# Attention scores from raw fp32 keys and queries, two heads on row halves, and all softmax weights turned as fp32r

## The chip, the cores and the metric

The kernel runs on one core of one Trainium2 chip. The metric is the device time in microseconds (us), the median of three runs. The kernel before takes 802.15 us (801.47 to 803.35).

## The reference

Three layers follow one another; everything is float32.

```python
# attention: batch 2, 8 heads, 576 tokens, head size 64
scores = scale * np.matmul(q, k.transpose(0, 1, 3, 2))
kth = np.partition(scores, -32, axis=-1)[..., -32:-31]     # the 32nd largest of each row
scores = np.where(scores >= kth, scores, -1e9)
attn = softmax(scores)                                     # written out in the reference
x = np.matmul(attn, v)                                     # then as 1152 tokens x 512
# experts: 4 of them, 512 -> 1024 -> 512
out += p[:, e:e+1] * (np.maximum(x @ w1[e], 0.0) @ w2[e])
# gated layer: 512 -> 1536 (twice) -> 512
y = ((x @ w_a) * (x @ w_b)) @ w_out
```

## The kernel before, in words

**Tokens.** The 1152 tokens are nine tiles of 128: four of each batch element, and one mixed tile with the last 64 tokens of both. `GROUPS` cuts the nine tiles into groups of 1, 2, 3 and 3; the last group holds two plain tiles and the mixed one. A group's attention runs over four pairs of heads, so there are 36 steps n = 0 to 35, each one tile with two heads; group 1 is n = 4 to 11, group 2 is n = 12 to 23, group 3 is n = 24 to 35.

**One step of attention.** `scores` (line 874) multiplies queries by keys into PSUM. ScalarE copies the scores to SBUF. `masked` (line 908) finds the 32nd largest of each row on VectorE: four MAX8 and three MATCH_REPLACE8 for each head (lines 930 and 936), all of 576 columns. ScalarE makes the softmax (lines 960, 965, 976) in a tile `e`. `weigh` (line 983) turns the weights on TensorE, nine 128x128 transposes a step, ScalarE copies them out, and when the last tile of a pair of heads is there, TensorE multiplies them by V (line 1033): ten pairs of matmuls a tile, the two heads of a pair on column halves of the array.

**Number formats.** A plain fp32 matmul is split into two instructions by the compiler, an fp32r one is a single instruction. Before the change the scores use fp32r. Keys and queries are split into a high part (ScalarE, line 623) and a remainder (GpSimd or VectorE, lines 625 and 627); both parts stand in the 128 rows of the array for one head, turned by fp32r transposes, and each query tile is multiplied twice, the second time with its halves swapped (`qa` and `qb`). So a plain tile has eight matmuls of 288 columns a step, and the mixed tile sixteen, with `qm` as its padded queries. The weights of steps n < 24 are turned in fp32. Those of n = 24 to 35 (`MOVED`) are first copied by DMA into an fp32r tile (`ers`) and turned there.

**The layers behind attention.** Group 0 goes through the experts in plain fp32 (`plain`), the others in a high and low split (`experts`, lines 1100 and 1115: in the trace `ps<-xs,mid_again` for the first matrix and `ps<-mid_again` for the second). Each weight unit is split by `w_unit`: ScalarE makes the high part (line 1073); the remainder comes from GpSimd, or from VectorE where `late` says so (lines 1076 and 1078):

```python
            late = 2 if c == len(GROUPS) - 1 and e >= 2 else 0
...
            lo = vector(dve(1024), lambda: sub(nc.vector), 500 + s if late > 1 else -100, [hi], [u, r], port=True)
        else:
            lo = gpsimd(pool_(1024), lambda: sub(nc.gpsimd), -100, [hi], [u, r])
```

The gated layer follows when all groups are through.

**What sets the order.** Every operation is given to a planner (`Plan`) with an engine, a duration and a key. The planner plays the whole program through with these durations, picks on each engine the ready operation with the smallest key, and the result is one fixed order for each engine. Score and attention work has keys near n, expert work has keys from 1000, evictions and remainders have negative keys. An engine then runs its list strictly in order. All transfers are issued by SyncE.

Of the kernel before, what the change touches and what calls it, by code (L numbers as in the profile page):

```python
# [21 lines left out]
MIX = "mix"  # L22
# [9 lines left out]
STORED, STORE_AT, STORE_KEY = 3, 10, 2.5  # L32
MOVED = (*range(24,36),)
# [43 lines left out]
class Buffer:  # L77
    def __init__(self, slots, need):
        self.slots, self.need, self.slot, self.users = slots, need, None, 0

    @property
    def ap(self):
        a = self.slots.aps[self.slot]
        return a[0][a[1]] if isinstance(a, tuple) else a

# [29 lines left out]
class Plan:  # L115
# [82 lines left out]
    def order(self):  # L198
# [34 lines left out]
        def place(t):  # L233
# [3 lines left out]
            if t.n != s.next:  # L237
                return None
            for i in sorted(s.free):
# [17 lines left out]
        def pick(engine):  # L257
# [6 lines left out]
            while ready_:  # L264
# [4 lines left out]
                ok = y is None or free[y.engine] <= now  # L269
                for t in op.tiles:  # L270
                    if t.slot is None and (t.slots in stuck or place(t) is None):
                        if t.n == t.slots.next:
                            stuck.add(t.slots)
                        ok = False
                if ok:
# [108 lines left out]
TURN_R, TURN_F, TOP, REPLACE = 88, 109, 662, 732  # L384
AV, SWITCH = 1092, 350

# [15 lines left out]
def body(tc, q, k, v, probs, w1, w2, wa, wb, wo, out):  # L402
# [58 lines left out]
    qm = const("qm", [128, 2, 2, 2, 128], F32R)  # L461
# [6 lines left out]
    kscr = dr.tile([B, HP, 2 * D, 2, S], F32, name="kscr")  # L468
    qscr = dr.tile([len(SIZES), HP, 2 * D, 2 * 3 * 128], F32, name="qscr")
    wscr = dr.tile([F2 // 256, 128, 2048], F32, name="wscr")  # L470

    big = Region("big", 10752, F32R)
    krems = big.slots("krem", 1, 1024)
    kspls = big.slots("kspl", 1, 2 * M4 * 2 * D)
    big.at = 2304
    bts = big.slots("bt", 4, 2 * S)
    qspls = big.slots("qspl", 1, 2 * 3 * 2 * D)
    qas = big.slots("qa", 2, 2 * 3 * 128)
    qbs = big.slots("qb", 1, 2 * 3 * 128)
    qts = big.slots("qt", 1, 2 * 3 * 128)  # L480
    big.at = 0
    ers = big.slots("er", 2, 2 * S)
    ers.rank = 0.5
# [10 lines left out]
    low = Region("low", 9228 + 3 * DM, F32)  # L494
    kraws = low.slots("kraw", 2, 2 * M4 * D)
    vts = low.slots("vt", 4, 2 * M4 * D)
    qraws = low.slots("qraw", 1, 2 * 3 * D)
    es = low.slots("e", 3, 2 * S)
# [4 lines left out]
    krraws = kraws  # L503
    low.at = 9228
# [3 lines left out]
    low.at = 9228  # L508
# [4 lines left out]
    big.again()  # L513
# [4 lines left out]
    ress.append(low.slots("res2", 1, DM))  # L518
    draws = low.slots("draw", 2, 1024)
    dcs = low.slots("dc", 2, 512)  # L520
# [1067 lines left out]
```

## Time and profile before

| | |
|---|---|
| median of the runs | 802.15 us (801.47 to 803.35) |
| profiled execution | 803.23 us, of which the span 801.2 us |
| mean granted TensorE clock | 0.987 |
| PE busy | 776.7 us, 97% |
| DVE busy | 706.7 us, 88% |
| ACT busy | 526.0 us, 66% |
| POOL busy | 338.0 us, 42% |
| chain that ended last | PE 67%, DVE 23%, ACT 4% |

The span is what the profiler saw on the core; 2.0 us of the profiled time lie around it. PE is TensorE, DVE VectorE, ACT ScalarE, POOL GpSimd, SP SyncE with the DMA queue. A PE row's length covers overlapping matmuls and a modelled end, so the real step of a PE group is read from its start to the start of the next group.

### The profile page before, as it was taken

The page shows a single profiled execution, that of the slowest core. Times are in us where ns is not written, and L with a number is a line of the kernel's source. Part 1 is how long each engine was busy: PE and PEld are TensorE (multiplying, and loading weights), DVE is VectorE, ACT ScalarE, POOL GpSimd, SP SyncE. Part 2 cuts the span into 40 slices and gives each one's busy share as a digit, 9 for nine tenths or more (in the row PEclk, how much of TensorE's full clock was granted, in tenths as well). Part 3 has the DMA queues.
Part 4 walks back from the last instruction along what each step waited for, and adds up shares of the span by engine and source line. Part 5 has one row for each costly group of instructions (what it writes and reads, how often), then busy time and mean ns, then how long its engine had stood idle before and what let it go on. Part 6 is the DMA issues. An engine that isn't in the chain of part 4 may idle for free.

```text
span 801.2 us, 14455 instructions
## 1 busy us (share of the span) xinstructions
PE 776.7 (97%) x5221; PEld 702.3 (88%) x5221; DVE 706.7 (88%) x1398; ACT 526.0 (66%) x926; POOL 338.0 (42%) x318
## 2 busy tenths in 40 slices
PE   6699999999999999999999999999999999999998
PEld 5587787799999989999999998999898989899996
DVE  7999999999999999999943676789788989999965
ACT  5899888999989898977774545566554533334210
POOL 4312113566765734535364656422224334333320
PEclk8799999999999999999999999999999999999999
DMA  5987997957657575763445544598631313304013
GB/s 170 328 278 228 301 313 238 271 187 248 211 173 227 178 216 172 227 191 129 145 154 168 185 129 147 158 324 296 223 142 54 106 53 106 131 28 158 1 53 119
DMA packets 98008, 143.57 MB, mean 179 GB/s; under 512 B 11792, under 2 KB 66064, under 8 KB 96400
## 3 DMA queue, kind: packets, MB, share of 16 engines
q1 hardware_dynamic: 97936, 142.65, 54.9%
q8 instruction: 41, 0.67, 0.3%
q14 instruction: 31, 0.25, 0.1%
HBM read 117.46 MB, written 14.42 MB: 165 GB/s over the span
## 4 chain that ended last, share of the span: by engine, by line
PE 67%; DVE 23%; ACT 4%; issue 3%; DMA 2%; POOL 1%; POOLq 0%; SPq 0%; DVEq 0%
PE ps L569 64%; DVE low L930 10%; DVE low L936 9%; PE ps L572 3%; DVE mid_again L1146 1%; DMA big<-big 1%; ACT low L965 1%; DVE low L1171 1%; ACT low L960 1%; POOL mid_again L1074 0%; DMA low<-in_v_dram 0%; ACT big L623 0%; ACT lowa L903 0%; POOL big L627 0%; DVE xs L1052 0%
## 5 line engine op out<-in xcount | busy, mean ns | idle before, releaser
L569 PE MATMUL ps<-mid_again 128*128 128x512 f32 x1092 | 261.7, 392 | 0.0
L569 PEld LDWEIGHTS ps<-mid_again 128*128 128x128 f32 x1092 | 201.5, 188 | 38.9 <-ACT raw L1521 0.2
L1074 POOL TENSOR_TENSOR mid_again<-raw,mid_again 128x1024 fp32r<-128x1024 f32 x80 | 192.6, 2418 | 65.8 <-ACT mid_again L1073 64.3
L569 PE MATMUL ps<-xs,mid_again 128*128 128x384 f32 (+1 forms) x1152 | 194.1, 320 | 0.1
L569 PEld LDWEIGHTS ps<-xs,mid_again 128*128 128x128 f32 x1152 | 182.4, 189 | 2.4 <-issue 0.5
L930 DVE MAX8 low<-low 128x8 f32<-128x576 f32 x216 | 154.5, 750 | 0.0
L1073 ACT ACTIVATE mid_again<-raw 128x1024 fp32r<-128x1024 f32 x96 | 101.1, 1063 | 32.4 <-PE ps L569 20.3
L936 DVE MATCH_REPLACE8 low<-low 128x576 f32<-128x576 f32 x144 | 106.5, 746 | 0.0
L1390 POOL TENSOR_TENSOR low<-low 128x512 int32<-128x512 int32 x36 | 50.7, 1407 | 116.6 <-DVE low L1387 80.9
L569 PE MATMUL ps<-xs,big 128*128 128x320 f32 (+1 forms) x576 | 86.4, 297 | 0.0
L569 PEld LDWEIGHTS ps<-xs,big 128*128 128x128 f32 x576 | 80.2, 190 | 0.8
L1146 DVE SCALAR_TENSOR_TENSOR mid_again<-ps,mid_again 128x384 fp32r<-128x384 f32 (+1 forms) x96 | 48.5, 508 | 32.9 <-ACT mid_again L1142 32.7
L569 PE MATMUL ps<-lowa_again,big 128*128 128x320 f32 (+1 forms) x432 | 66.4, 297 | 0.8 <-ACT rest L1488 0.6
L1142 ACT ACTIVATE mid_again<-ps 128x384 fp32r<-128x384 f32 (+1 forms) x96 | 44.0, 458 | 32.7 <-PE ps L569 29.9
L569 PEld LDWEIGHTS ps<-lowa_again,big 128*128 128x128 f32 x432 | 60.6, 190 | 2.2 <-ACT rest L1488 0.9
L960 ACT ACTIVATE low<-lowa,low 128x576 f32<-128x576 f32 x72 | 54.4, 781 | 4.7 <-POOL low L950 4.6
L976 ACT ACTIVATE low<-low 128x576 f32<-128x576 f32 x72 | 53.5, 778 | 5.1 <-DVE low L973 4.6
L965 ACT ACTIVATE low<-low 128x576 f32<-128x576 f32 x72 | 56.1, 783 | 0.2 <-POOL low L954 0.2
L936 DVE MATCH_REPLACE8 low<-low,lowa 128x576 f32<-128x576 f32 x72 | 53.2, 746 | 0.0
L1016 ACT ACTIVATE lowa<-ps 128x512 f32<-128x512 f32 x72 | 46.3, 654 | 9.4 <-PE ps L572 8.9
L930 DVE MAX8 low<-lowa 128x8 f32<-128x576 f32 x70 | 50.0, 748 | 0.7 <-ACT lowa L903 0.7
L1479 DVE TENSOR_TENSOR low<-ps,low 128x256 f32<-128x256 f32 (+1 forms) x105 | 43.2, 445 | 7.6 <-PE ps L569 6.5
(121 smaller groups left out, 1115.8 us busy)
## 6 DMA issues: line engine op xcount, KB each, us to landing
raw<-in_moe_w_dram SPq DMA_DIRECT2D x116, 512.0 KB, 4.1
big<-kscr SPq DMA_DIRECT2D x20, 576.0 KB, 5.0
big<-low SPq DMA_DIRECT2D x24, 288.0 KB, 3.3
low<-in_v_dram SPq DMA_DIRECT2D x24, 256.0 KB, 3.8
low<-in_moe_w_b_dram SPq DMA_DIRECT2D x12, 512.0 KB, 3.7
low<-in_moe_w_a_dram SPq DMA_DIRECT2D x12, 512.0 KB, 3.6
low<-in_moe_w_out_dram SPq DMA_DIRECT2D x12, 512.0 KB, 4.4
wscr<-big SPq DMA_DIRECT2D x6, 1024.0 KB, 5.9
```

The lines of the kernel that those rows point to most:

```text
L569: nc.tensor.matmul(out, l, r, **kw)
L930: 62 + 1.04 * width, lambda at=at, cs=cs: nc.vector.max(m8v()[:, x, cs], at()), key + 0.02 * r, [done],
L936: lambda at=at, cs=cs: nc.vector.match_replace(out=src[1](), in_to_replace=m8v()[:, x, cs], in_values=at(), imm_value=LOW),
L960: S, lambda x=x, s=s: nc.scalar.activation(ev(x), s.ap, AF.Prelu, bias=endv()[:, x, 1:2], scale=scale, alpha=STEEP),
L965: lambda x=x: nc.scalar.activation(ev(x), ev(x), AF.Exp, bias=endv()[:, x, 0:1], accum_out=sums.ap[:, x:x + 1]),
L976: S, lambda x=x: nc.scalar.activation(ev(x), ev(x), AF.Copy, scale=sums.ap[:, x:x + 1]),
L1016: w, lambda j=j, w=w, at=at: nc.scalar.activation(p.ap[:, j * MAIN:j * MAIN + w], at.ap.rearrange("p b n -> p (b n)")[:, j * (MAIN - 128): ...
L1073: hi = scalar(1024, lambda: nc.scalar.activation(u.ap[:, 0:1024], r.ap, AF.Copy), 500 + s, [ld], [u, r], sbuf=True)
L1074: sub = lambda eng: eng.tensor_tensor(u.ap[:, 1024:2048], r.ap, u.ap[:, 0:1024], op=ALU.subtract)
L1142: n, lambda h=h, p=p: nc.scalar.activation(h.ap[:, 0:n], p.ap[:, 0:n], AF.Relu), -1000, [o], [h, p]
L1146: lambda h=h, p=p: nc.vector.scalar_tensor_tensor(h.ap[:, n:2 * n], p.ap[:, 0:n], 0.0, h.ap[:, 0:n], op0=ALU.max, op1=ALU.subtract),
L1390: return gpsimd(pool_(512), lambda: nc.gpsimd.tensor_tensor(t().bitcast(I32), fold(c.ap.bitcast(I32)), fold(lowv().bitcast(I32)), op=ALU.a ...
```

## The change

- Keys and queries are no longer split. The raw keys of a pair of heads are loaded side by side, turned by six plain fp32 transposes a block, and evicted in one copy: head 0 stands in rows 0 to 63, head 1 in rows 64 to 127. Queries are turned in the same way, one transpose a tile.
- `scores` makes both heads in one step: four fp32 matmuls of 288 columns, each on one row half. In the mixed tile each is cut once more into two 64-column halves, one for each batch element: eight matmuls.
- All 36 steps' weights are turned as fp32r. The tile `e` is asked for a second time at the same address with the type fp32r (`Typed`); a GpSimd memset of one column behind its end stands for the new tile's write, and the transposes wait for it. The copies of `MOVED`, the mirrored queries and the stored queries go.
- `late`: VectorE makes the weight remainders of all of group 3 and of experts 2 and 3 of group 2; in all 48 of 96 instead of 16 of 96.

```diff
-MOVED = (*range(24,36),)
...
+LATE = 2
...
+    def keys(b, h2, key):
...
+        for m0, m1 in ((0, 2), (2, M4)) if first_ else ((0, M4),):
+            for i in range(2):
+                lds.append(load(
+                    lambda i=i, m0=m0, m1=m1: rv()[:, m0:m1, i], lambda i=i, m0=m0, m1=m1: main_rows(k, b, h)[:, i, m0:m1],
+                    key - 2, (), [rt], 32768 * (m1 - m0),
+                ))
+        if first_:
+            for c in range(B):
+                for x in range(B):
+                    rs = slice((x + c) % B * REM, ((x + c) % B + 1) * REM)
+                    krem_done.append(load(
+                        lambda c=c, rs=rs: krem[c].ap[rs].rearrange("p (h d) -> p h d", d=D), lambda x=x: last_rows(k, x), key - 1.98, (), [krem[c]], 131072,
+                    ))
...
+            tr(a[:, 0:128], kr[0], ident)
+            for m in range(M4):
+                tr(a[:, (1 + m) * 128:(2 + m) * 128], rt.ap[:, m * 128:(m + 1) * 128], ident)
+            tr(a[:, 640:768], kr[1], ident)
+
+        o = tensor(6 * TURN_F, turn, key + 0.02, lds + krem_done + [ready], [at, rt] + krem)
...
+            for i, t in enumerate(pair.tiles):
+                tr(a()[:, i * 128:(i + 1) * 128], qrem[:, h:h + 2].rearrange("p h d -> p (h d)") if t == MIX else rq.ap[:, i * 128:(i + 1) * 128], ident)
...
+        parts = [(slice(0, 128), t[0])] if t != MIX else [(slice(b * REM, (b + 1) * REM), b) for b in range(B)]
...
             for c in range(2):
-                for m_, (a, kt) in enumerate(parts):
-                    for lh in range(2):
+                for j in range(2):
+                    for rs, b in parts:
+                        c0 = (1 - j) * REM + c * HALF
                         mm(
-                            at.ap[:, c, 0:HALF], pair.qv(j, i, lh) if a is None else a[:, lh], kt[:, c * HALF:(c + 1) * HALF],
-                            start=(m_ + lh == 0), stop=(m_ == len(parts) - 1 and lh == 1),
+                            ats[j].ap[rs, c, 0:HALF], pair.q.ap[j * D:(j + 1) * D, i * 128 + rs.start:i * 128 + rs.stop],
+                            pair.k[b].ap[j * D:(j + 1) * D, c0:c0 + HALF], start=True, stop=True,
                         )
...
-        if n in MOVED:
-
-            f, idt = ers.tile(n), identr
-            done = [load(
-                lambda j=j: f.ap[:, j * S:(j + 1) * S].bitcast(F32), lambda j=j: e.ap[:, j * S:(j + 1) * S], n + 0.1, [done[j]], [e, f], S * 512,
-            ) for j in range(2)]
+        turnable = []
+
+        def retype():
+            a = e.slots.aps[e.slot]
+            t_ = a.tile(F32R)
+            turnable[:] = t_, nc.gpsimd.memset(t_[:, a.words:a.words + 1].bitcast(F32), 0.0).ins
+
+        typed = gpsimd(90, retype, -4500, done, [e])
...
+                    made.append(tr(a[:, j * MAIN + m * 128:j * MAIN + (m + 1) * 128], f[:, c0:c0 + 128], identr))
...
-            late = 2 if c == len(GROUPS) - 1 and e >= 2 else 0
+            late = 2 if c == len(GROUPS) - 1 else c == len(GROUPS) - 2 and e >= LATE
...
-        sd = [scores(pair, j, i, n) for j in range(2)]
+        sd = scores(pair, i, n)
```

SyncE's list at the start of the program, before the change (`low` and `big` are regions of SBUF):

```order
L551 DMA low<-in_k_dram 128x2x256
L551 DMA low<-in_k_dram 64x2x64
L551 DMA low<-in_q_dram 128x2x64
L551 DMA low<-in_k_dram 64x6x64
L551 DMA low<-in_k_dram 128x2x256
```

The same list of the changed kernel:

```order
L571 DMA big<-in_k_dram 128x2x64 x4
L571 DMA big<-in_k_dram 64x8x64 x4
L571 DMA big<-in_q_dram 128x64 x2
L571 DMA big<-in_k_dram 128x4x64 x2
L571 DMA big<-in_q_dram 128x64 x2
```

The first scores stood behind three transfers and now stand behind ten.

TensorE's list around group 2's last multiplication by V, before (`ps<-lowa` is that multiplication, 64x128 the column halves; `ps<-big` are plain scores, `ps<-big,qm` mixed ones; 384 columns belong to group 2's experts):

```order
L569 MATMUL ps<-xs,mid_again 128x384 x6
L572 MATMUL ps<-identr,low 128x128 x9
L569 MATMUL ps<-xs,mid_again 128x384 x6
L569 MATMUL ps<-big,qm 128x288 x8
L569 MATMUL ps<-lowa,low 64x128 x8
...
L569 MATMUL ps<-lowa,rest 64x128 x2
L569 MATMUL ps<-big,qm 128x288 x8
L572 MATMUL ps<-identr,big 128x128 x2
L569 MATMUL ps<-xs,mid_again 128x384 x12
L572 MATMUL ps<-identr,low 128x128 x8
```

The same place of the changed kernel (`e_18_2619` is the retyped weight tile):

```order
L589 MATMUL ps<-xs,mid_again 128x384 x18
L592 MATMUL ps<-identr,low 128x128 x8
L592 MATMUL ps<-identr,e_18_2619 128x128 x9
L589 MATMUL ps<-xs,mid_again 128x384 x9
L589 MATMUL ps<-lowa,low 64x128 x8
...
L589 MATMUL ps<-lowa,rest 64x128 x2
L589 MATMUL ps<-big 64x288 x8
L589 MATMUL ps<-xs,mid_again 128x384 x6
```

27 of group 2's first matmuls stand ahead of the multiplication where 12 did, and group 1's last eight transposes (`identr,low` x8) moved ahead of it. All of group 1's expert matmuls stand ahead of it in both lists.

TensorE's list around the last multiplication by V of all, before:

```order
L572 MATMUL ps<-identr,big 128x128 x5
L569 MATMUL ps<-mid_again 128x512 x6
L569 MATMUL ps<-lowa,low 64x128 x8
...
L569 MATMUL ps<-lowa,rest 64x64 x2
L569 MATMUL ps<-mid_again 128x512 x27
L569 MATMUL ps<-xs,mid_again 128x384 x48
L569 MATMUL ps<-mid_again 128x512 x36
```

The same place of the changed kernel:

```order
L592 MATMUL ps<-identr,e_28_4131 128x128 x9
L589 MATMUL ps<-mid_again 128x512 x6
L589 MATMUL ps<-lowa,low 64x128 x8
...
L589 MATMUL ps<-lowa,rest 64x64 x2
L589 MATMUL ps<-mid_again 128x512 x9
L589 MATMUL ps<-xs,mid_again 128x384 x24
```

Of group 2's experts 63 matmuls of 512 columns and 48 of 384 stood behind this place; 9 of 512 columns are left there.

## Rows read from the trace of the kernel before

**Rows 1.** Busy time by stage: PE, PEld, DVE, ACT, POOL, then granted clock, DMA share, GB/s

```profile
40.00:276.70 236.70, 231.40 (x1783) 201.36 (x1782) 234.72 (x515) 216.01 (x396) 113.25 (x118) 0.99 0.76 238
320.00:400.00 80.00, 80.00 (x616) 73.72 (x613) 78.67 (x164) 64.52 (x116) 35.66 (x35) 1.00 0.55 176
```

**Rows 2.** Chain that ended last, in order of time: start us, us, what

```profile
284.22 0.48 DVE mid_again L1146
284.74 0.66 PE ps L572 x4
...
608.18 189.15 PE ps L569 x1194
```

**Rows 3.** Timeline of the start, SP and DVE; then landing of the first query loads

```profile
0.72 1.26 SPq L551 DMA_DIRECT2D low<-in_k_dram  x2
...
2.65 3.39 SPq L551 DMA_DIRECT2D low<-in_k_dram  x2
...
8.12 1.66 DVE L925 MAX8 low<-ps 128x8 f32<-128x576 f32 x2 [0.70 <-PE ps L569]
...
low<-in_q_dram SPq DMA_DIRECT2D x2, 64.0 KB, 2.4
```

**Rows 4.** Timeline of PE: plain fp32 matmuls, and fp32 turns

```profile
47.91 1.05 PE L569 MATMUL ps<-xf,mid 128*128 128x128 f32 x8
48.80 1.15 PE L572 MATMUL ps<-identr,low 128*128 128x128 f32 x9
49.79 0.61 PE L569 MATMUL ps<-xf,mid 128*128 128x128 f32 x4
...
77.44 1.02 PE L569 MATMUL ps<-raw,low 128*128 128x512 f32 x2
78.30 0.71 PE L572 MATMUL ps<-identr,low 128*128 128x128 f32 x5
```

**Rows 5.** Timeline of PE around group 2's last multiplication by V

```profile
275.50 1.23 PE L569 MATMUL ps<-big,qm 128*128 128x288 f32 x8
276.66 1.09 PE L569 MATMUL ps<-lowa,low 128*64 128x128 f32 x16
...
277.80 1.04 PE L569 MATMUL ps<-lowa,low 128*64 128x128 f32 x16
...
278.89 1.04 PE L569 MATMUL ps<-lowa,low 128*64 128x128 f32 x16
...
280.08 1.34 PE L569 MATMUL ps<-big,qm 128*128 128x288 f32 x8
```

**Rows 6.** Timeline of PE, plain scores of one head in group 3

```profile
325.85 0.70 PE L569 MATMUL ps<-big 128*128 128x288 f32 x4
326.38 0.69 PE L569 MATMUL ps<-xs,mid_again 128*128 128x384 f32 x3
```

**Rows 7.** Timeline of PE towards the last multiplication by V

```profile
397.72 7.52 PE L569 MATMUL ps<-xs,mid_again 128*128 128x384 f32 x42
405.07 2.24 PE L569 MATMUL ps<-mid_again 128*128 128x512 f32 x9
407.15 0.46 PE L572 MATMUL ps<-identr,big 128*128 128x128 f32 x4
407.45 0.93 PE L569 MATMUL ps<-mid_again 128*128 128x512 f32 x3
...
425.48 1.09 PE L569 MATMUL ps<-lowa,low 128*64 128x128 f32 x16
```

**Rows 8.** End of attention on DVE and ACT; remainders on DVE; copies of `MOVED`

```profile
406.27 0.75 DVE L930 MAX8 low<-low 128x8 f32<-128x576 f32 x1
...
415.32 1.43 ACT L976 ACTIVATE low<-low 128x576 f32<-128x576 f32 x2
...
L1074 DVE TENSOR_TENSOR mid_again<-raw,mid_again x16: 1208/1218/2049, 514.1 to 570.5; 128x1024 fp32r<-128x1024 f32 x16
...
big<-low SPq DMA_DIRECT2D x24, 288.0 KB, 3.3
```

More of the change, by code (lines that the diff above doesn't have):

```diff
@@ L236, in place @@
                 return t.slot
-            if t.n != s.next:
+            mine = [i for o, i in claimed if o is s]
+            if t.n != s.next + len(mine):
                 return None
-            for i in sorted(s.free):
+            for i in sorted(s.free.difference(mine)):
                 if s.spans is None:
@@ L795, in queries @@
                     qrem_done.append(load(lambda b=b: qrem[b * REM:(b + 1) * REM], lambda b=b: last_rows(q, b), key - 2, (), (), 131072, since=60e3))
-            more.append(lambda sqv: split(
-                lambda: sqv()[:, :, m, 0], lambda: sqv()[:, :, m, 1], lambda: qrem[:, h:h + 2], 2 * D, key + 0.03, qrem_done, [sq], "POOL"
-            ))
-        if kept_ is None or more:
-            rq, sq = qraws.tile(key) if kept_ is None else None, qspls.tile(key)
-            rqv, lds = fetch(pair.tiles, h, key, rq) if kept_ is None else (None, [])
@@ L836, in start_pair @@
+        pair.q = qa
     def start_pair(c, h2, n):
@@ L872, in start_pair, with scores @@
         return pair
-    def scores(pair, j, i, n):
+    def scores(pair, i, n):
         t = pair.tiles[i]
-        at, s = atts.tile(n - AHEAD), ss.tile(n)
-        if t == MIX:
-            bs = list(range(B))
-            after = pair.md + sum((pair.kd[b][j:j + 1] for b in bs), [])
-            used = [pair.k[b] for b in bs]
-        else:
-            bs = [t[0]]
-            after = pair.qd[j] + pair.kd[t[0]][j:j + 1]
-            used = [pair.k[t[0]]] + pair.q
+        ats, ss_ = [atts.tile(n - AHEAD + 0.001 * j) for j in range(2)], [ss.tile(n + 0.001 * j) for j in range(2)]
+        parts = [(slice(0, 128), t[0])] if t != MIX else [(slice(b * REM, (b + 1) * REM), b) for b in range(B)]
@@ new lines, in scores @@
+        o = tensor(SCORE / 2 + TILED, emit, n - AHEAD, pair.qd + sum((pair.kd[b] for _, b in parts), []), ats + [pair.q] + [pair.k[b] for _, b in parts])
+        got = []
+        for j in range(2):
+            at, s = ats[j], ss_[j]
+            ev = scalar(
+                S, lambda s=s, at=at: nc.scalar.activation(s.ap.rearrange("p (c n) -> p c n", c=2), at.ap[:, :, 0:HALF], AF.Copy),
+                -2000 + n, [o], [at, s],
+            )
+            got.append((s, ev, at, o))
+        return got
```

332 lines of the change are left out of this document (99 added, 233 removed).

## The prediction, made before the changed kernel ran

> **What bounds the kernel now.** I read the page first: PE is busy for 97% of the span and DVE for 88%, so neither total says which of them ends the program. The chain of waits does. Its early part is mostly DVE with the top-32 search; at 284.7 us it leaves DVE for PE [rows 2], and from there to the end it is PE but for a short stretch before the piece that starts at 608. So there are two stages. Before 284.7 the attention loop on DVE sets the pace: DVE is busy for 234.72 of the 236.70 us from 40 to 276.7 [rows 1], and PE, busy for 231.40 of them, takes expert work whenever it has nothing of attention to do. Expert work that can be taken forward is limited: all matmuls of group 1's experts stand ahead of group 2's last multiplication by V, and that multiplication needs the last step of group 2 from DVE. After 284.7 PE's own work is the bound: PE is busy for all of the 80 us of a late window in which DVE has gaps [rows 1]. A microsecond of PE work saved before that point is therefore worth something only if PE uses it for work from behind the point; saved behind it, it counts in full, as long as attention is not late.
>
> **What the change does to PE's operations.** Each duration is a distance from start to start.
>
> Weights: nine fp32 turns take 48.80 to 49.79, 0.99 us [rows 4]. Four fp32r turns take 407.15 to 407.45, 0.30 us [rows 7], so nine are estimated at 0.68. The change saves 0.31 in each of 24 steps, 7.4 us. All 24 are in groups 0 to 2; group 3 is turned as fp32r already.
>
> Plain scores: one head's four fp32r matmuls take 0.53 us [rows 6], two heads 1.06. In fp32 each matmul is two instructions. Two such instructions of 512 columns take 77.44 to 78.30, 0.43 each [rows 4]; scaled to 288 columns that is an estimate of 0.242. A step has eight of them: 1.94 us one after the other. No row shows two row halves at work together. The nearest row is the multiplication by V on two column halves: 20 instructions of mostly 128 columns take 277.80 to 278.89, 1.09 us [rows 5], while plain 128-column fp32 instructions take 0.89 for eight, 0.111 each, 2.22 for twenty [rows 4]. The pairs overlap by a factor of 2.04. Going into and out of the split array costs the difference between the first and last tile there (1.14 and 1.19) and the middle one (1.09): 0.05 and 0.10 [rows 5]. The bounds of a score step are thus 0.97 + 0.15 = 1.12 us with full overlap and 1.94 + 0.15 = 2.09 without. I take 1.12, from the nearer row. Against 1.06 before that is a loss of 0.06 a step.
>
> Mixed scores: one head takes 275.50 to 276.66, 1.16 us [rows 5], a step 2.32. The eight small matmuls of the changed step sit on the four quarters of the array; by the same row they overlap, and I again take 1.12 (bounds 1.12 and 2.09). Saving 1.2 a step.
>
> Keys and queries: six fp32 turns of 0.11 replace eight fp32r ones of about 0.075 and two small matmuls for each of eight key blocks, and one fp32 turn replaces two fp32r ones for each query tile. Both are within 0.1 us of nothing apiece and nearly all lie ahead of 284.7.
>
> **What of it reaches the end.** Term 1, the start. Before, the first score waits for three loads; SP issued them from 0.72, and four issues bring it a bit past 2.65, so one takes 0.64 [rows 3]. Now ten loads stand first: the last is issued at 0.72 + 9 x 0.64 = 6.5 and lands 2.4 later [rows 3], at 8.9. One turn, one copy and a score step follow: about 0.2, 0.4 and 1.1, with semaphores between them some 11.1. The first MAX8 started at 8.12 [rows 3]. Against this stands that no split is done any more; it is in the sum, since the turn follows the landing directly. The loss is 3.0 us, and as the DVE loop starts that much later with a full load, it passes on to group 2's last multiplication. Bounds: 1.0, if the 2.0 us of gaps that DVE has on the way close [rows 1], and 4.0, if the first score step takes 2.09 and not 1.12.
>
> Term 2, work taken forward. 24 weight turns, keys and queries free about 8 us of PE before that multiplication. The order shows what it takes forward with them: 27 instead of 12 of group 2's 384-column matmuls, 15 x 0.175 (42 take 397.72 to 405.07 [rows 7]) = 2.6 us, and eight turns at 0.11, 0.9 us. Together 3.5. The other 4.5 us become waiting time of PE and are worth nothing.
>
> Term 3, work saved behind it. Before, seven half steps of mixed scores follow, 7 x 1.16 = 8.1; now four whole steps, 4 x 1.12 = 4.5: a gain of 3.6. Six plain steps lose 6 x 0.06 = 0.4. Queries lose 0.1. Sum: a gain of 3.1.
>
> Term 4, attention's end. 16 remainders more come to DVE while it still searches for group 3, 1.22 us each [rows 8], 19.5 us. With the 3.0 of the start the search, whose last MAX8 began at 406.27, ends some 22.5 later. The copy of `MOVED` at 3.3 [rows 8] is gone from the path behind it, so the last multiplication by V may start 19.2 us later than now. Before, the chain ran through PE there and the scaling on ACT that ended at 416.75, plus 3.3, came 0.9 ahead of the turn that PE reached at about 420.9, so 0.9 of slack is to be had. PE itself reaches this multiplication later by the work moved ahead of it: 54 matmuls of 512 columns at 0.231 (nine in 405.07 to 407.15 [rows 7]) and 48 of 384 at 0.175, 20.9 us, plus 3.0, less terms 2 and 3, 6.6: 17.3 us later than 425.48 [rows 7]. 19.2 against 17.3 + 0.9 leaves PE waiting for 1.0 if all 16 come before the last search, and for nothing if 15 do: I take 0.5. Bounds: nothing, and 5, as the experts' evictions for the work moved ahead are on DVE too.
>
> The GpSimd memset stands behind remainders of that engine; what is queued behind it are the small sums of the next step, and DVE waits for none of them as long as three weight tiles are in turn. I cost it at nothing; if the cover is gone, one remainder of delay in the last step of a group falls on the path, inside the bounds of term 4. The smaller traffic (no copies, no mirrored queries) is worth nothing by itself, as DMA does not stand in the chain after 284.7.
>
> Sum: + 3.0 - 3.5 - 3.1 + 0.5 = - 3.1 us. The profiled execution took 803.23 and would take 800.1; it lies 1.1 above the median of the runs, 802.15, from which the same sum gives **799.0 us**.
>
> **Rivals.** (a) The row halves overlap only in part. For it: no row shows them, and the two heads write four PSUM banks in turn. Against it: the column halves overlap fully. Halfway, at 1.6 us a step, ten steps behind the multiplication cost 10 x 0.48 = 4.8 more: 803.8; at a quarter of the way 801.4. The Trainium skill (TensorE: Matmul & The Clock Gate, section Measured speedup vs the span model) gives 3.07 for four row tiles, which by estimate leaves a pair at 1.53 and a score step at 1.94/1.53 + 0.15 = 1.42; the sum would be 3 us more, 802.0. No run here shows row tiles yet; the column halves at 2.04 speak against it.
>
> (b) They do not overlap at all: 2.09 us a step, ten steps behind cost 9.7, and the 26 ahead cost 25 us of PE that has 8 to spare there, so some 10 to 17 more go past the handover: 809 to 826, slower than before. A step decides at about 1.4 us; above it the gain is gone.
>
> (c) DVE becomes the bound of group 3: the remainders and evictions move the search's end by 25 to 30 us instead of 22.5, and PE, which has only nine matmuls of group 2 left behind the last multiplication, waits for it one to one. For it: DVE is busy for 78.67 of 80 us there [rows 1]. Against it: DVE had gaps after the search. It is slower than before from a wait of 5.2 us on; at 6 us of wait the time is 804.5.
>
> (d) The start costs little, since gaps on DVE close, and the waits go with the copies: 1.0 instead of 3.0 in term 1 and nothing in term 4 gives 796.5.
>
> **How the numbers follow.** The forecast has 0.55 (its own range 797 to 801), (a) 0.16, (b) 0.05, (c) 0.13, (d) 0.11. The range is 795 to 805: it takes in (d), (c) at its price and most of (a), and leaves out (b) and the far ends. About 0.2%, 1.6 us, is what a measurement here tells from no change: faster is below 800.5, slower above 803.8. Faster: 0.50 of the forecast's 0.55, all of (d), 0.02 of (a): 0.63. Slower: (b), 0.07 of (c), 0.04 of (a): 0.16. The same: the rest, 0.21.
>
> **What would show it.** The first MAX8 at about 11 us. A mixed and a plain score step both at 1.1 us from start to start, two heads together; a step near 2 makes (b) true. All weight turns at about 0.68 a step. PE waiting before group 2's last multiplication, where it did not. The chain changing from DVE to PE a little later than 284.7 and staying on PE; if DVE's search stands in it between 400 and 450, (c) is true. The last multiplication by V at 442 to 444. The forecast is wrong if the time is above 801 or below 797.

## The result, and the profile after

The changed kernel takes 808.49 us (808.02 to 810.65); before took 802.20 beside it. The ratio is 1.0082, with a 95% interval of 1.0060 to 1.0104: it is slower by 4.8 to 8.3 us, where the prediction had 799.0 and a range up to 805. The profiled execution took 808.02, its span is 806.2. It is the fastest of its four runs, so the two traces differ by 5.0 us where the medians differ by 6.3; the accounts below divide up the 5.0.

Busy time by stage, in the columns of [rows 1]; the first row ends at group 2's last multiplication by V, as there:

```profile
40.00:285.70 245.70, 234.16 (x1765) 190.13 (x1764) 242.54 (x531) 211.19 (x379) 103.01 (x129) 0.99 0.61 193
...
320.00:400.00 80.00, 80.00 (x633) 68.97 (x631) 78.58 (x153) 59.34 (x101) 20.38 (x29) 1.00 0.37 121
```

VectorE is as full as before. TensorE is idle for 11.5 us of the first stretch, where it had been idle for 5.3, and never between 320 and 400.

The chain that ended last, at the places of [rows 2]:

```profile
293.10 0.47 DVE mid_again L1031
...
293.61 0.79 PE ps L589 x3
...
610.32 192.04 PE ps L589 x1218
```

The chain leaves VectorE at 293.1 where it left it at 284.2: the handover is 8.9 us later. From there to the end it is shorter by 3.8 (to 802.36, before to 797.33). 8.9 less 3.8 is, but for rounding, the 5.0 by which the span grew. The handover is where VectorE's eviction (L1146 before, L1031 after) releases TensorE, which stays in the chain from there on: at 284.74 before and 293.61 after.

The start, SyncE's queue, TensorE and VectorE, against [rows 3]:

```profile
0.71 4.80 SPq L571 DMA_DIRECT2D big<-in_k_dram  x8
...
8.45 1.73 PE L592 MATMUL ps<-identr,big 128*128 128x128 f32 x7 [4.16 <-DMA big<-in_k_dram]
10.88 2.29 PE L589 MATMUL ps<-big 64*128 64x288 f32 x8 [0.70 <-DVE big L726]
...
13.17 1.43 DVE L804 MAX8 low<-ps 128x8 f32<-128x576 f32 x2 [2.44 <-PE ps L589]
```

The keys and queries have landed by 8.45. Then seven turns take 1.73, the copies 0.70 and the eight score instructions 2.29, so the first MAX8 comes at 13.17 and not at 8.12: 5.05 later.

VectorE from its first MAX8 to the handover, before and after, in the columns of [rows 1], and its evictions of 512 columns into `xs` in these stretches:

```profile
8.12:284.74 276.62, 259.15 (x1987) 225.36 (x1986) 274.51 (x600) 247.03 (x462) 125.64 (x142) 0.96 0.77 244
L1278 DVE TENSOR_TENSOR xs<-ps,xs 128x512 fp32r<-128x512 f32 x1 | 0.7, 668 | 0.0
...
13.17:293.61 280.44, 257.57 (x1933) 207.36 (x1932) 277.23 (x604) 232.31 (x421) 104.57 (x138) 0.99 0.63 198
L1163 DVE TENSOR_TENSOR xs<-ps,xs 128x512 fp32r<-128x512 f32 x3 | 2.0, 678 | 0.0
```

VectorE works for 277.23 us there instead of 274.51, and is idle for 3.21 instead of 2.11. With the 5.05 of the start, 2.7 of work and 1.1 of waiting make up the 8.9. Most of the added work is two evictions of eight turns that were taken forward, and one MAX8 (207 instead of 206).

Turns and scores in the middle of the program, against [rows 4 to 6] (64x288 x8 is a plain step of two heads, 64*64 x16 a mixed one):

```profile
270.20 0.89 PE L592 MATMUL ps<-identr,e 128*128 128x128 f32 x9
270.93 1.62 PE L589 MATMUL ps<-mid_again 128*128 128x512 f32 x6
272.47 1.24 PE L589 MATMUL ps<-big 64*128 64x288 f32 x8
273.64 2.34 PE L589 MATMUL ps<-mid_again 128*128 128x512 f32 x9
...
289.13 1.20 PE L589 MATMUL ps<-big 64*64 64x288 f32 x16
290.26 0.44 PE L589 MATMUL ps<-xs,mid_again 128*128 128x384 f32 x1
```

From start to start a step's nine turns take 0.73, a plain step of scores 1.17, a mixed one 1.13.

Group 2's last step, from the scaling on ScalarE over GpSimd to TensorE:

```profile
278.36 4.69 POOL L959 TENSOR_TENSOR mid_again<-raw,mid_again 128x1024 fp32r<-128x1024 f32 x2 [0.73 <-ACT mid_again L958]
283.00 0.09 POOL L874 MEMSET e<- 128x1 f32 x1
...
280.10 1.43 ACT L855 ACTIVATE e<-e,low 128x576 f32<-128x576 f32 x2
...
283.15 0.97 PE L592 MATMUL ps<-identr,e 128*128 128x128 f32 x9 [1.50 <-POOL e L874]
...
285.70 1.09 PE L589 MATMUL ps<-lowa,low 128*64 128x128 f32 x16
```

The scaling ends at 281.53; the memset stands behind two remainders until 283.00. The multiplication by V starts at 285.70, 9.04 later than in [rows 5].

The last multiplication by V, against [rows 7, 8]:

```profile
447.80 0.10 POOL L874 MEMSET e<- 128x1 f32 x1 [4.05 <-ACT e L855]
448.47 0.87 PE L592 MATMUL ps<-identr,e 128*128 128x128 f32 x9
...
450.73 1.09 PE L589 MATMUL ps<-lowa,low 128*64 128x128 f32 x16
...
438.65 0.75 DVE L809 MAX8 low<-e 128x8 f32<-128x576 f32 x1
```

The search ends 32.4 us later than before and the multiplication starts 25.3 later. The turn at 448.47 has no wait in front of it, but the memset that it needs had ended only 0.6 before.

### The profile page after: what moved, and what is told of

Same layout as the page of the kernel before. It is cut to its first block, busy times and chain, and to the rows that moved or that the text cites. A ratio compares the mean times of both kernels' runs of the same rounds, so it can differ in the third digit from the quotient of the medians.

```text
span 806.2 us, 14094 instructions
## 1 busy us (share of the span) xinstructions
PE 771.0 (96%) x5145; PEld 673.1 (83%) x5145; DVE 731.9 (91%) x1425; ACT 508.0 (63%) x871; POOL 238.0 (30%) x289
## 4 chain that ended last, share of the span: by engine, by line
PE 87%; DVE 7%; DMA 2%; ACT 1%; SPq 1%; issue 0%; POOL 0%; DVEq 0%; ACTq 0%
PE ps L589 83%; PE ps L592 4%; DVE low L809 3%; DVE e L815 2%; DMA mid<-in_moe_w_dram 2%; SPq L571 1%; ACT lowa L901 0%; DMA big<-in_k_dram 0%; DVE mid_again L1031 0%; DVE xs L1163 0%; DVE low L1056 0%; ACT big L686 0%; ACT e L855 0%; ACT lowa L781 0%; DVE e L1272 0%
## 5 line engine op out<-in xcount | busy, mean ns | idle before, releaser
L809 DVE MAX8 low<-e 128x8 f32<-128x576 f32 x216 | 154.5, 748 | 0.0
L959 POOL TENSOR_TENSOR mid_again<-raw,mid_again 128x1024 fp32r<-128x1024 f32 x48 | 114.8, 2402 | 25.5 <-ACT mid_again L958 23.2
L815 DVE MATCH_REPLACE8 e<-low,e 128x576 f32<-128x576 f32 x144 | 106.1, 743 | 0.0
L589 PE MATMUL ps<-xs,big_again 128*128 128x320 f32 (+1 forms) x576 | 86.4, 297 | 0.2 <-DVE low L1364 0.2
L589 PEld LDWEIGHTS ps<-xs,big_again 128*128 128x128 f32 x576 | 80.3, 190 | 1.1 <-DVE low L1364 0.4
L589 PE MATMUL ps<-lowa_again,big_again 128*128 128x320 f32 (+1 forms) x432 | 66.4, 296 | 1.4 <-ACT rest L1373 1.1
L959 DVE TENSOR_TENSOR mid_again<-raw,mid_again 128x1024 fp32r<-128x1024 f32 x48 | 62.2, 1301 | 5.0 <-ACT mid_again L958 4.8
L589 PEld LDWEIGHTS ps<-lowa_again,big_again 128*128 128x128 f32 x432 | 60.8, 190 | 2.5 <-ACT rest L1373 1.3
L839 ACT ACTIVATE e<-lowa,low 128x576 f32<-128x576 f32 x72 | 53.1, 776 | 13.7 <-POOL low L829 13.3
L855 ACT ACTIVATE e<-e,low 128x576 f32<-128x576 f32 x72 | 52.7, 772 | 11.1 <-DVE low L852 11.0
L844 ACT ACTIVATE e<-e,low 128x576 f32<-128x576 f32 x72 | 55.6, 775 | 0.8 <-POOL low L833 0.7
L1031 DVE SCALAR_TENSOR_TENSOR mid_again<-ps,mid_again 128x384 fp32r<-128x384 f32 (+1 forms) x96 | 48.3, 506 | 7.4 <-ACT mid_again L1027 6.7
L1364 DVE TENSOR_TENSOR low<-ps,low 128x256 f32<-128x256 f32 (+1 forms) x105 | 43.7, 447 | 11.4 <-PE ps L589 10.8
```

The source lines that it names most:

```text
L589: nc.tensor.matmul(out, l, r, **kw)
L809: 62 + 1.04 * width, lambda at=at, cs=cs: nc.vector.max(m8v()[:, x, cs], at()), key + 0.02 * r, [done],
L815: lambda at=at, cs=cs: nc.vector.match_replace(out=src[1](), in_to_replace=m8v()[:, x, cs], in_values=at(), imm_value=LOW),
L839: S, lambda x=x, s=s: nc.scalar.activation(ev(x), s.ap, AF.Prelu, bias=endv()[:, x, 1:2], scale=scale, alpha=STEEP),
L844: lambda x=x: nc.scalar.activation(ev(x), ev(x), AF.Exp, bias=endv()[:, x, 0:1], accum_out=sums.ap[:, x:x + 1]),
L855: S, lambda x=x: nc.scalar.activation(ev(x), ev(x), AF.Copy, scale=sums.ap[:, x:x + 1]),
```

## The experiments

The theory first: the late start is the loss, because the search on VectorE carries it to the handover one to one (A). Rivals: the hop over GpSimd, that is the memset in front of the weight turns (C), the remainders on VectorE (term 4), the written order (D), later SyncE's queue (E) and late expert weights (F). All but e4 and the replanned runs keep the order of the changed kernel. The differences are to the kernel before in the same comparison; the changed kernel stands at + 6.3, and its own executions spread from 808.02 to 810.65.

| run | edit | median, us | to before | ratio, 95% |
|---|---|---|---|---|
| e1 | other start loads | 805.15 | + 3.1 | 1.0023 to 1.0051 |
| e2 | longer warm-up | 807.26 | + 5.2 | 1.0056 to 1.0081 |
| e3 | retype on ScalarE | 813.48 | + 11.4 | 1.0127 to 1.0174 |
| e4 | order from other draws | 809.69 | + 7.6 | 1.0083 to 1.0110 |
| e5 | e1, first head first | 805.80 | + 3.8 | 1.0033 to 1.0058 |
| e6 | fp32 turns in groups 0 to 2 | 812.21 | + 10.2 | 1.0119 to 1.0150 |
| e7 | retype on VectorE at three places | 809.55 | + 7.6 | 1.0082 to 1.0110 |
| e8 | 16 remainders back | 809.90 | + 7.9 | 1.0087 to 1.0115 |
| e9 | replanned | 806.62 | + 4.6 | 1.0038 to 1.0064 |
| e10 | e1, replanned | 802.75 | + 0.7 | 1.0004 to 1.0021 |
| e11 | before, replanned | 804.65 | + 2.6 | 1.0017 to 1.0039 |
| e12 | e1, second head's loads on GpSimd | 806.64 | + 4.4 | 1.0029 to 1.0062 |
| e13 | e12, replanned | 803.76 | + 1.5 | 1.0006 to 1.0025 |
| e14 | e13 with 70 ns | 808.91 | + 6.6 | 1.0062 to 1.0091 |
| e15 | e1, weights early by GpSimd | 816.46 | + 14.4 | 1.0164 to 1.0195 |
| e16 | e10, weights early by GpSimd | 811.61 | + 9.6 | 1.0107 to 1.0134 |
| e17 | e10, weights together by SyncE | 802.69 | + 0.2 | 0.9994 to 1.0011 |
| e18 | e13, weights together by SyncE | 803.94 | + 1.5 | 1.0008 to 1.0032 |

**e1, the start loads.**

```diff
-key - 2, (), [rt], 32768 * (m1 - m0),
+key - 2, (), [rt], 32768 * (m1 - m0), by=nc.scalar if first_ and i else nc.sync,
-lambda c=c, rs=rs: krem[c].ap[rs]..., lambda x=x: last_rows(k, x), ...
+lambda c=c, rs=rs: krem[c].ap[rs]...[:, 0:2], lambda x=x: last_rows(k, x)[:, 0:2], ..., by=nc.scalar if x else nc.sync,
```

> The changed kernel with another start and nothing else moved: of the ten loads ahead of the first turn, those of the second head and of the second batch's remainder rows are issued by ScalarE instead of SyncE, and the remainder loads bring only the first two heads (the other six heads follow behind the loads of the next key block). Theory A (the lost time is the late start, carried one to one by the search on VectorE): five issues of 0.6 us a queue instead of ten end near 3.7 instead of 6.65 and 0.83 MB become 0.45 MB, so the first MAX8 starts near 10 instead of 13.17, the handover from VectorE to TensorE (293.6) comes 3 earlier, and the time is about 805.5. Rival B (the start is absorbed by gaps on the way, the loss lies in the handover and in the order): the first MAX8 moves as well, but the time stays within 1 us of 808.5.

VectorE at its start:

```profile
9.71 1.43 DVE L811 MAX8 low<-ps 128x8 f32<-128x576 f32 x2 [2.44 <-PE ps L589]
```

The first MAX8 is 3.46 earlier and the time 3.2 to 3.3 lower. Theory A holds for this part, and 3.1 us of the loss remain. In the traces of the changed kernel and of the nine runs that keep its order (e1 to e3, e5 to e8, e12, e15) VectorE works for 277.2 to 277.7 us from the first MAX8 to the handover, and from there to TensorE's end it takes 508.6 to 510.1. What differs is when the search starts and how long VectorE waits on the way.

**e2, the cold start.**

```diff
-lambda: mm(idle.ap[:, 0:256], ...)
+lambda i=i: [mm(idle.ap[:, 0:256], ...) for _ in range(15 if i == FILL - 1 else 1)]
```

> The changed kernel with 14 more idle matmuls behind the nine at the start, so that TensorE is busy until the first keys land, and nothing else moved. Theory A with a cold array as one of its parts: the first eight score matmuls take 1.2 us instead of 2.29 and the seven turns ahead of them 0.8 instead of 1.73, the first MAX8 starts near 11.3 instead of 13.17, and the time is about 806.6. If the rate at the start does not hang on what TensorE did before, both durations stay, and the time stays at 808.5. If the idle matmuls run past the landing of the keys they add up to 0.5.

```profile
2.01 5.27 PE L589 MATMUL ps<-xs 128*128 128x256 f32 x23 [2.01 <-DVE xs L1417]
8.42 0.96 PE L592 MATMUL ps<-identr,big 128*128 128x128 f32 x7 [1.14 <-DMA big<-in_k_dram]
10.39 1.68 PE L589 MATMUL ps<-big 64*128 64x288 f32 x8 [1.01 <-DVE big L726]
...
12.04 1.43 DVE L804 MAX8 low<-ps 128x8 f32<-128x576 f32 x2 [1.79 <-PE ps L589]
...
10.40:12.10 1.70, 1.67 (x8) 0.81 (x8) 0.06 (x1) 0.00 (x0) 0.00 (x0) 0.69 0.71 161
```

The turns fall from 1.73 to 0.96, the scores only to 1.68: TensorE had been idle for 1.14 and 1.01 us ahead of them, and while they run the granted clock is 0.69 on the mean, between its two levels, and then 0.50 (1.2 GHz) from 12 to 38. The first MAX8 is 1.13 earlier where 1.9 were expected, and the time falls by 1.1 to 1.2. So TensorE's slow rate is part of the start.

**e3 and e7, the hop.**

```diff
-nc.gpsimd.memset(t_[:, a.words:a.words + 1].bitcast(F32), 0.0)                                   # e3
+nc.scalar.activation(t_[:, a.words:a.words + 1], facs, AF.Copy)
-nc.gpsimd.memset(...)                                                                            # e7
+(nc.vector if n in (3, 11, 23) else nc.gpsimd).memset(...)
```

> The changed kernel with the one-column write that gives the softmax weights their new type on ScalarE, directly behind the scaling that it follows, instead of on GpSimd; nothing else moved. Theory C (the hop over GpSimd costs at group 2's end): from the last reciprocal of group 2 to its weight turn it takes 1.7 us instead of 3.6, the last multiplication by V of group 2 starts 1.9 earlier than 285.70, and the time is about 806.6. Theory A alone: the multiplication moves, but TensorE then waits for VectorE's evictions, which come no earlier, and the time stays within 0.7 of 808.5. 36 writes of about 0.2 us on ScalarE cost nothing in either.

> The changed kernel with the one-column write on VectorE instead of GpSimd in the last steps of groups 0, 1 and 2 only; all else as it was. In group 2's last step it stood 1.4 us behind a remainder on GpSimd. Theory C: the weight turn of that step starts 1.4 earlier, and the time is about 807.2. If VectorE has to wait for ScalarE's scaling at that place, the search is late by as much, and the time is 808.5 or somewhat above.

Group 2's last step in e3, then in e7:

```profile
284.10 1.43 ACT L855 ACTIVATE e<-e,low 128x576 f32<-128x576 f32 x2
...
286.19 0.20 ACT L874 ACTIVATE e<-facs 128x1 fp32r<-128x1 f32 x1
286.43 0.97 PE L592 MATMUL ps<-identr,e 128*128 128x128 f32 x9 [0.78 <-ACT e L874]
```

```profile
281.39 1.43 ACT L855 ACTIVATE e<-e,low 128x576 f32<-128x576 f32 x2
...
284.82 0.06 DVE L874 MEMSET e<- 128x1 f32 x1
...
288.98 1.13 PE L589 MATMUL ps<-lowa,low 128*64 128x128 f32 x16
```

Neither gains, and only e3 shortens the hop. There the write waits behind an eviction and comes 0.66 after the scaling's end, where it came 1.47 after. From group 2's last reciprocal to the turn it takes 2.96 us instead of 3.67, but from that reciprocal to the handover 14.1 in both kernels: in the changed kernel the chain is VectorE's alone from 279.6 to 293.6, so the hop is not on it. The run is 5 us slower all the same, 3.4 of it since VectorE waits for 6.6 us ahead of the handover instead of 3.2; that this comes of the extra work on ScalarE is likely but not shown. e7 is no test of a shorter hop: VectorE reaches the write 2.0 after the scaling's end, and from the reciprocal to the multiplication, at 288.98, it takes 8.2 us instead of 6.2.

**e4, other draws.**

```diff
-draw = random.Random(r)
+draw = random.Random(r + 1000)
```

> The changed kernel whose order is planned from other random draws; every instruction is there, some stand elsewhere. It measures how much of a difference the order alone makes. If the loss is in the change (theories A and C): within 1.5 us of 808.5, with the first MAX8 at 13.2 again. If the order of the changed kernel is an unlucky one: 803 or less.

The first MAX8 stays at 13.2 and the time is 1.3 higher, with an interval that overlaps the changed kernel's: other draws of the planner do no better.

**e5, the first head first.**

```diff
-for c in range(2):
-    for j in range(2):
+for c, j in ((0, 0), (1, 0), (0, 1), (1, 1)) if n == 0 else ((0, 0), (0, 1), (1, 0), (1, 1)):
```

> The kernel of the run with the other start loads, and in the first step alone the four score matmuls of the first head stand ahead of those of the second, so that VectorE need not wait for both. Theory A: the eight matmuls take 2.29 us together and the first head's now 1.2, so the first MAX8 starts near 8.6 instead of 9.7, and the time falls by the same 1.1 from 805.15, to about 804.0. If the search catches up in a gap behind (VectorE has few there), it stays at 805.

```profile
7.78 2.30 PE L589 MATMUL ps<-big 64*128 64x288 f32 x8 [0.70 <-DVE big L733]
...
10.07 1.43 DVE L811 MAX8 low<-ps 128x8 f32<-128x576 f32 x2 [2.44 <-PE ps L589]
```

A miss: the eight instructions start in pairs in this order too, and VectorE waits as long for them as in e1. (An instruction's row does not name its head, so whether the written order was also that of the issue is not shown.) The first MAX8 is 0.36 later since the loads landed later; the time is 0.7 higher, with overlapping intervals.

**e6, one part undone.**

```diff
+if n < 24:      # fp32 turns straight from e, no memset
+    tr(a[:, j * MAIN + m * 128:j * MAIN + (m + 1) * 128], e.ap[:, c0:c0 + 128], ident)
```

> The changed kernel with the softmax weights of groups 0 to 2 turned in fp32 again, straight from their tile, without the write on GpSimd; group 3 as changed; the order is kept. It takes back one part of the change: 24 x 0.31 = 7.4 us more on TensorE ahead of the handover, where TensorE waited for some 8 us from 140 to 300, and no hop over GpSimd. Theory C (the hop is what costs at group 2's end): the time falls by up to 1.4 us, to 807. If the TensorE work saved there was worth what the prediction gave it (3.5 us in this group of terms), the time rises to 811 or more. Theory A alone (the start is everything, the turns are hidden): 808.5 within 0.7.

VectorE from the first MAX8 to the handover in this run:

```profile
13.10:296.57 283.47, 262.70 (x1931) 211.02 (x1931) 277.53 (x604) 233.65 (x421) 103.04 (x114) 1.00 0.63 196
```

It costs 3.9 us, and the faster turns are thus worth something, though TensorE has idle time ahead of the handover. That this is near the 3.5 of term 2 is luck, as it comes by another path: from the handover to the end nothing changes (508.75), while VectorE is idle for 5.9 us instead of 3.2 ahead of it, waiting above all for outputs of TensorE.

**e8, the remainders.**

```diff
-lo = vector(dve(1024), lambda: sub(nc.vector), ...
+lo = vector(dve(1024), lambda: sub(nc.vector if late > 1 else nc.gpsimd), ...
```

> The changed kernel with the 16 weight remainders of group 2's last two experts on GpSimd again (2.4 us each there, 1.22 on VectorE); the order is kept. Term 4 and rival (c) of the prediction: if VectorE's extra 19.5 us between 290 and 450 delayed the end of attention, the time falls by up to 5 us. Theory A: TensorE was busy without a gap from 300 to 460, so nothing is to be had: 808.5 within 0.7, with the last MAX8 up to 19 us earlier than 438.7; above that if TensorE waits for weights from GpSimd.

The chain of this run near 395:

```profile
395.27 2.37 POOL mid_again L959
397.63 0.11 POOL e L874
...
397.78 0.95 PE ps L592 x9
```

Nothing is gained. From 320 to 400 VectorE is now idle for 9.2 us (1.4 in the changed kernel), but the last MAX8 begins at 442.57 and not earlier, as GpSimd stands in the chain; the memset behind a remainder delays TensorE by 0.4 between 300 and 400. So the run does not bring the search's end forward; it shows that giving VectorE less work there gains nothing.

**e9, e10 and e11, the order.** The same three numbers in each (110 instead of 70 in e10, which has e1's loads):

```diff
-SEEN, SEEN_PE = 45, 130
+SEEN, SEEN_PE = 70, 130
-COLD, COLD_END = 1.2, 46e3
+COLD, COLD_END = 1.6, 38e3
-ISSUE, LAND, GBS, LANES = 500, 2700, 320.0, 8
+ISSUE, LAND, GBS, LANES = 600, 2700, 320.0, 8
```

> The changed kernel with the same instructions in an order that is planned with longer times between engines: 70 ns instead of 45 from the end of an instruction until another engine sees it, 600 instead of 500 ns for issuing a load, and a slower TensorE in the first 38 us (factor 1.6 instead of 1.2). Theory D (besides the start, the written order is the loss: it puts VectorE's evictions where their matmuls are not yet done, nine waits of 0.23 to 0.88 between 14 and 300 us, 3.6 us together, and leaves TensorE without work for 4.4 us from 140 to 180 and 4.0 from 260 to 300): these waits fall below 1.5 us together, the handover comes some 3 earlier, and the time is 803 to 806. Theory A alone (the start sets it): 808.5 within 1.5, like the order from other draws (809.7).

> Both edits together: the loads of the start on two queues with the remainder rows of two heads first, and the order planned for that, with the longer times (110 ns here, 600 ns, factor 1.6). Theories A and D add up: 3.3 from the start and 3 to 5 from the order, so 800 to 802, below the kernel before. If the order is worth nothing, it stays at 805.2, as with the loads alone.

> The kernel before, with its order planned with the same longer times as the first of these three runs. Control for theory D: VectorE waits for only 2.1 us between 14 and 300 there, so little is to be had: 802.0 within 1.5. If the longer times help every kernel alike, it falls by as much as the changed one, to 799 or less, and theory D says nothing about the change.

The order gives 1.7 and, with the other start, 2.4; for the kernel before it costs 2.6. But VectorE's waits did not shrink in e9 and e10 (one at 88 us is 1.3 in e9, one at 85 is 1.4 in e10), so these three do not show theory D's mechanism.

**e12, e13 and e14, SyncE's queue.**

```diff
+by=(nc.scalar if first_ else nc.gpsimd) if i else nc.sync,        # keys of the second head
+by=(nc.gpsimd if n else nc.scalar) if i and n < 5 else nc.sync,   # its queries
```

> The kernel with the other start loads (order kept), and in addition the loads of every second head's keys, of its queries in the first five steps and of the other remainder rows are issued by GpSimd, which has nothing else to do there, instead of by SyncE. Theory E (the queue of SyncE is the second half of the loss: it has twice as many loads to issue, so the first expert weights come late and TensorE, in the chain from 46 us on, stays behind): some 12 issues of 0.5 us fewer stand ahead of the first expert weights, which are issued near 19 instead of 24, VectorE's waits on outputs at 104, 125 and 136 us (1.8 together) shrink to less than 0.6, and the time is 803 to 803.8 instead of 805.15. Rival D (the order is the rest): the weights come earlier, but the time stays at 805.2 within 0.6. If the transfers and not their issue are the limit, the first weights land no earlier than now.

> The same queues in an order planned for them, with the longer times (110 ns, 600 ns, factor 1.6), as in the run that took 802.75. Theories A, D and E together: 1.5 to 2 below that run, 800.7 to 801.3, and below the kernel before (802.04). If the queue was no cost, 802.7.

> The same as the run before it, planned with 70 ns instead of 110. Theory E: as that run within 1 us, 800 to 802, first MAX8 near 9.8. The difference between the two shows what the choice of an order alone moves.

VectorE's waits on the evictions into `xs` from 14 to 300 us, first in e13:

```profile
DVE xs L945 <- ACT xs L943: 0.4, 1, 0.4
```

then in e14:

```profile
DVE xs L945 <- ACT xs L943: 4.6, 5, 1.9
```

e12 does not test theory E: the first expert weights are issued at 25.68 and not near 19 (24.20 in e1), since SyncE, ahead of loads of keys, waits for turns for 11.8 us between 4 and 26. e13 is a miss: it was to be faster than e10 and is 1.0 slower. e13 and e14 have the same instructions and differ in one number of the planner, and by 5.1 us: this pair does show what theory D says, that an order can put VectorE's evictions where their inputs are not done. Over all its waits VectorE has 1.6 us there in e13 and 6.9 in e14. The changed kernel's idle time of VectorE is 1.1 us above that of the kernel before.

**e15 and e16, weights early.**

```diff
+then=(lambda: [nc.gpsimd.dma_start(out=o(), in_=i()) for o, i in early[:3]]) if x == 0 else lambda: None,
```

> The kernel with the other start loads (order kept), and in addition the first three loads of expert weights, 1 MB each, are issued together by GpSimd near 20 us, instead of by SyncE at 24.2 and 29 to 31. Theory F (the second half of the loss is TensorE's late weights: it waits for them near 40 us, stays in the chain until 141 and VectorE waits for its outputs): the wait of 0.77 goes, TensorE's piece of the chain starts up to 2 earlier, VectorE's waits at 104, 125 and 136 shrink, and the time is 803.5 to 804.5 instead of 805.15. If the transfers then delay key and query loads beside them, the search waits for scores, and the time is above 805.5. Rival D (the order is the rest): 805.2 within 0.5.

> The kernel that took 802.75 (other start loads, replanned), in the same order, with the same early issue of the three weight loads. There TensorE waits 2.8 us for the second load and VectorE 1.49 at 85 us for an output. Theory F: both waits go and the time falls by 1.5 to 2.5, to 800.3 to 801.3, faster than the kernel before. Rival D: 802.7 within 0.6.

GpSimd in e15, and who waited (us in total, times, longest):

```profile
20.42 0.98 POOL L1199 DMA_DIRECT2D mid<-in_moe_w_dram  x1
29.10 0.77 POOL L1199 DMA_DIRECT2D mid<-in_moe_w_dram  x1 [7.70 <-issue]
37.69 0.76 POOL L1199 DMA_DIRECT2D mid<-in_moe_w_dram  x1 [7.82 <-issue]
38.52 0.22 POOL L856 TENSOR_SCALAR low<-low 128x2 f32<-128x2 f32 x1
...
DVE low L859 <- POOL low L856: 10.8, 1, 10.8
```

The three issues held GpSimd until 38.5, and the softmax sums stood behind them. As a test of the weights both runs failed; for theory A they are the strongest rows: 10.8 us of wait in the search and 11.3 us more time in e15, 9.3 and 8.9 in e16.

**e17 and e18, weights together, by SyncE.**

```diff
-then=(lambda: [nc.gpsimd.dma_start(out=o(), in_=i()) for o, i in early[:3]])
+then=(lambda: [nc.sync.dma_start(out=o(), in_=i()) for o, i in early[:3]])
```

> The kernel that took 802.75 (other start loads, replanned), same order on the four engines; on SyncE the second and third load of expert weights stand directly behind the first, at 24 us instead of 28.8, ahead of some key and query loads. Theory F: TensorE's wait of 2.77 at 41 us falls below 1, VectorE's wait of 1.49 at 85 us shrinks, and the time is 800.8 to 801.8, below the kernel before. Rival G (the transfers fill the DMA engines from 24 to 51 us anyway, so what comes earlier makes something else late): keys or queries behind them land later, the search or TensorE waits for these, and the time is 802.7 or more.

> The same edit on the kernel that took 803.76 (second head's loads on GpSimd, replanned), whose wait for weights at 41 us is 1.33 and where VectorE has no wait at 85 us. Theory F: 802.5 to 803.5. Rival G: 803.8 or more.

VectorE's longest wait from 60 to 160, first in e10:

```profile
DVE xs L945 <- ACT xs L943: 1.8, 2, 1.4
```

then in e17:

```profile
DVE xs L945 <- ACT xs L943: 0.4, 1, 0.4
```

The wait for late weights goes as theory F says, but the time falls by 0.5 at most, and in e18 not at all. e17 is the best version found and is level with the kernel before; none beats it.

## Why the prediction was wrong

The sum had - 3.1 us and the traces differ by + 5.0. Of these 8.1 us, term 1 lacked 2.05, 3.8 stood in no term, and terms 2 to 4 brought some 2.2 less than forecast.

**Term 1, the start, is the first step that failed.** It had the first MAX8 at 11.1, and it came at 13.17: + 5.05 and not + 3.0, beyond its upper bound of 4.0. The landing was nearly right (8.9 forecast, 8.45 measured). What follows was not: "about 0.2, 0.4 and 1.1" for one turn, one copy and a score step are 1.73, 0.70 and 2.29. Two things are wrong in it. There are seven turns ahead of the first scores, not one; and both they and the scores ran at half the rate that the middle of the program shows (0.11 a turn, 1.17 a step). The first slip is hidden by luck: 8.45 with seven turns of 0.11, 0.70 and 1.17 gives 11.09, the forecast's number, so practically all of the 2.05 is the slow rate, of which e2 took back 1.13. The upper bound had a score step of 2.09, for want of overlap and not for a slow rate. That the delay passes on one to one was right and is shown four times: - 3.46 gave - 3.2 (e1), - 1.13 gave - 1.1 (e2), + 10.8 gave + 11.3 (e15) and + 9.3 gave + 8.9 (e16).

**Between the start and the handover 3.8 us more were lost that no term held.** Ahead of the handover the prediction charged VectorE with its late start alone. It gained from work taken forward (term 2) and did not charge that work's evictions to VectorE, which has no gap for them: 2.7 us more of VectorE's own work stand there, for the most part two such evictions and one MAX8, and it waits 1.1 us longer. By the time of group 2's last reciprocal (279.48, before 271.83) 2.6 of the 3.8 are lost. The memset, costed at nothing with "one remainder of delay in the last step of a group" as its price if the cover is gone, did lose its cover: the turn comes 3.7 us after the reciprocal instead of 1.6. That is not part of the loss, since the chain there runs through VectorE; shortening it moved nothing (e3). Another order takes back some 2 (e9, e10), earlier weights at most 0.5 (e17). No run takes the added evictions away with all else kept, so the 2.7 and 1.1 are read from the traces and not shown by an experiment.

**Terms 2 to 4 were - 6.1 and came to - 4.0**, from group 2's last multiplication by V to the end (520.7 before, 516.7 after). Each group counted from start to start over that stretch: Term 2: 27 matmuls and the eight turns stand ahead as the order showed, but the fifteen matmuls are worth 1.6 where 2.6 were forecast (each of the rest takes 0.1765 instead of 0.175), the turns 1.0 against 0.9. Term 3: 4 x 1.13 and 6 x 1.17 are 11.5 where 7 x 1.16 and 6 x 1.06 were 14.5, a gain of 2.9 against 3.2; over all score groups of that stretch it is 3.3. Against it, group 3's weight turns, which the prediction left as they were, take 0.081 each instead of 0.074, and with the query turns that is 1.1 us where 0.1 was charged. Term 4: TensorE did not wait for the last turn, but elsewhere behind the multiplication, for 2.2 us in all, 1.4 before: 0.8 against 0.5.

**The rivals.** (a) and (b) are out: 1.17 and 1.13 against the forecast of 1.12. The Trainium skill (TensorE: Matmul & The Clock Gate, section Measured speedup vs the span model), with its 3.07 for four row tiles, led by estimate to 1.42; for two row halves the trace differs from that estimate, and they overlap within 0.05 us of the forecast's full overlap. Four tiles of 32 rows no run here shows. (c) came true in its condition and not in its price: the search ends 32.4 us later, more than its 25 to 30, and the multiplication came at 450.73 and not at 442 to 444. But TensorE had become late as well, by the 8.9 of the handover, is busy without a gap from 320 to 450.73, and was spared the wait by 0.6 us; e8 gains nothing. (d) is out in its start, which was dearer; its other half holds, since TensorE did not wait for the last turn.

## What to carry to other kernels

When an engine is full from its first instruction on, every microsecond ahead of that instruction is a microsecond of the program: count each instruction of that path, at the durations which the first 20 us of the profile show and not those of its middle. Work of the other engine that is taken forward brings its evictions with it: charge them to the full engine. Work saved on the other engine ahead of the handover does not shorten the full engine's work, but it can spare it waits (e6). And an order made by a planner moved these kernels by 1 to 5 us by itself, so a change worth 3 needs a replanned control beside it.

## What the hardware showed beside it

- Two row halves overlap with one head's matmuls all written ahead of the other's as well: eight still took 2.30 (e5), as when they are interleaved (2.29).
- The granted clock of a row does not always show that TensorE is slow. From 8.4 to 38 us it reads 1.00 in the changed kernel and 0.54 in e2, and later score steps of that stretch take 2.29 in both, against 1.24 in the middle of the program. The first clock event in the changed kernel's trace is at 39.2 us, so the 1.00 ahead of it stands on no event. The changed kernel, then e2:

```profile
8.40:38.00 29.60, 18.11 (x81) 12.54 (x81) 25.43 (x55) 15.18 (x29) 1.25 (x7) 1.00 0.77 219
...
17.18 2.29 PE L589 MATMUL ps<-big 64*128 64x288 f32 x8 [0.75 <-ACT big L728]
```

```profile
8.40:38.00 29.60, 17.87 (x85) 12.36 (x87) 26.57 (x57) 15.46 (x30) 1.25 (x7) 0.54 0.81 228
...
16.04 2.29 PE L589 MATMUL ps<-big 64*128 64x288 f32 x8 [0.75 <-ACT big L728]
```

- Behind the issue of a 1 MB load, GpSimd came to its next issue 8.6 us later (e15) or 7.5 (e16), where issue to landing took 8.3 and 7.2; an instruction of another kind started 0.07 us after the third issue. SyncE takes 0.6 to 1.4 for an issue of such a load.
